# Attention stage of an attention, mixture-of-experts and MLP kernel: k laid out by depth, one product per pair of heads, and a new order of the stage

## The chip, the cores and the metric

The kernel runs on 1 core of one Trainium2 chip. The metric is the device time of one execution in microseconds (us). Engines have short names: PE is TensorE (PEld its weight loads), DVE is VectorE, ACT is ScalarE, POOL is GpSimd, SP is SyncE, which only issues transfers here.

## The reference, cut to what matters

```python
batch, n_heads, seq, head_dim = (8, 8, 576, 64)
...
def _attn_ref(q, k, v):
    q_s = np.exp(q - np.max(q, axis=-1, keepdims=True))
    q_s = q_s / (np.sum(q_s, axis=-1, keepdims=True) + 1e-09)
    k_s = np.exp(k - np.max(k, axis=2, keepdims=True))
    k_s = k_s / (np.sum(k_s, axis=2, keepdims=True) + 1e-09)
    kv = np.einsum('bhsd,bhse->bhde', k_s, v)
    return np.einsum('bhsd,bhde->bhse', q_s, kv)
...
x = attention output as 4608 tokens x 512
x = moe(x)        # 8 experts, each token goes to the one with the largest gate
out = moe2(x)     # 512 -> 2048 -> 512 with a leaky activation
```

q is normalised over the depth of a head (64), k over the sequence (576). The two large products after it (the experts, then the last MLP) take most of the time; the change touches the attention stage alone.

## The kernel before, in words

The attention stage is the function `attention`. Two batches make a pair, so there are 4 pairs of 1152 tokens, and a pair is 9 chunks of 128 tokens (4 of the first batch, 4 of the second, and one with the last 64 tokens of each). 8 heads of 64 are 4 pairs of heads (`hp`) of 128 columns. `j` is the batch inside the pair.

Per pair of batches the steps are these (lines of the kernel before). Loads: `load_k`, `load_v`, `load_q` (L125 to L138), on SP's queue, with tokens on the partitions. Maximum of k over the sequence: `kmax` (L149 to L151) takes elementwise maxima of the token chunks on DVE, `kmax_t` (L156) transposes the result on PE, `kmax_m` reduces it (L160) and makes diagonal matrices on ACT (L164), `kmax_b` multiplies by ones on PE (L170) so that every partition holds the maximum, copies it out on ACT (L172), and subtracts it from k in place, on POOL (L175, L176) but for one half of pair 0 on DVE. `kexp` (L180, L183) is exp on ACT in place. `kv` (L192) multiplies the five token chunks of a batch and a pair of heads with v; two columns of ones behind v give the sums. `kvn` (L198 to L207) divides by them and writes two diagonal blocks of 64x64 into a persistent tile `kvx`. `kvT` and `kg` (L214 to L224) multiply these blocks by the gate's weights, so that the gate's logits come out of the same product as the attention. For q: `qmax` (L245) and `qsub` (L249) by thirds of a pair, on DVE, the third `qsub` of pairs 1 to 3 on POOL. Per chunk: `trans` (four transposes L260, exp on ACT L262), `xmm` (product with `kvx`, L273 or L278, sums and logits taken out on ACT L280, L281, reciprocal on DVE L282), `evac` (division on DVE L287, store to `xd`). After a pair, `phase_r` finds each token's expert in 17 small steps r0 to r16 on DVE, and `scat` (L384) scatters a row per token into `region` with 36 indirect DMAs of POOL in all, 9 per pair (the last pair in 6 and 3).

The order of the stage is written out: every step has a due time in the table `TIMES`, a pair has a period of 12.5, the steps of all pairs are sorted by due time and issued in that order, and each engine works its own instructions in that order. The work on k's maximum, difference and exp for a pair lies two periods ahead of its x products, the products with v one period ahead.

After the stage `slot_tables` counts tokens per expert on DVE, `idload` (L552) reads the first 512 rows of `region`, which needs all scatters, and the experts begin.

```python
a1 += [at(i, f"kmax{j}", kmax, j), at(i, f"kmax_t{j}", kmax_t, j), at(i, f"kmax_m{j}", kmax_m, j),
       at(i, f"kmax_b{j}", kmax_b, j, eng)]
...
add(i - 2, a1)
add(i - 1, a2)
add(i - 1, phase_q(i))
add(i, phase_b(i))
...
for x in sorted(steps, key=lambda x: x[:2]):
    x[2](*x[3:])
```

Of the kernel before, what the change touches and what calls it, by code (L numbers as in the profile page):

```python
# [9 lines left out]
F32 = mybir.dt.float32  # L10
# [3 lines left out]
AF = mybir.ActivationFunctionType  # L14
# [8 lines left out]
NPAIR = B // 2  # L23
# [38 lines left out]
def lay_qk(a):  # L62
    r = np.ascontiguousarray(a.transpose(0, 2, 1, 3)).reshape(NT, DM)
    return np.ascontiguousarray(r[token_order()].transpose(0, 2, 1, 3))


def lay_v(a):
    r = a.transpose(0, 2, 1, 3).reshape(NPAIR, 2, S, 4, 128)
    o = np.zeros((NPAIR, 128, 2, 5, 4, 130), np.float32)
    for j in range(2):  # L70
        m = r[:, j, :512].reshape(NPAIR, 4, 128, 4, 128)
        o[:, :, j, :4, :, :128] = m.transpose(0, 2, 1, 3, 4)
        o[:, :, j, :4, :, 128:] = 1.0
        o[:, 64 * j:64 * j + 64, j, 4, :, :128] = r[:, j, 512:]
        o[:, 64 * j:64 * j + 64, j, 4, :, 128:] = 1.0
    return o
# [17 lines left out]
def attention(ctx, tc, cst, a, region, xd):  # L94
# [21 lines left out]
    T = cst["times"]  # L116

    def on(p, key, default):
        return {"p": nc.gpsimd, "v": nc.vector, "a": nc.scalar}[T.get((p, "E" + key), default)]

    def at(p, key, fn, *args):
        return (T.get((p, key), T[key]), fn) + args


    def load_k(i):  # L125
        t = kt[i] = kp.tile([128, NC, DM], F32, tag="k", name=f"k{i}")
        nc.sync.dma_start(out=t[:, 0:4], in_=a["k"][i, :, 0:4])
        nc.sync.dma_start(out=t[:, 4:9], in_=a["k"][i, :, 4:9])

    def load_v(i):  # L130
        t = vt[i] = kp.tile([128, 2, 5, 4, 130], F32, tag="v", name=f"v{i}")
        for j in range(2):
            nc.sync.dma_start(out=t[:, j], in_=a["v"][i, :, j])

    def load_q(i):
        t = qt[i] = kp.tile([128, NC, DM], F32, tag="q", name=f"q{i}")
        for c in range(0, 9, 3):
            nc.sync.dma_start(out=t[:, c:c + 3], in_=a["q"][i, :, c:c + 3])  # L138

    def phase_a(i):  # L140
# [3 lines left out]
        def kmax(j):  # L144
            pm2 = sp.tile([128, 2, DM], F32, tag="pm2", name="pm2", bufs=1)
            pm = s["pm", j] = sp.tile([128, DM], F32, tag="pm", name="pm")
            kj = kt[i][:, 4 * j:4 * j + 4]
            r = slice(64 * j, 64 * j + 64)
# [4 lines left out]
        def kmax_t(j):  # L153
            tp = s["tp", j] = ps_k.tile([128, 4, 128], F32, tag="kv", name="tp")
            for hp in range(4):
                nc.tensor.transpose(out=tp[:, hp], in_=s["pm", j][:, 128 * hp:128 * hp + 128], identity=ident)  # L156

        def kmax_m(j):
            m = sp.tile([128, 4], F32, tag="m", name="m")
            nc.vector.tensor_reduce(out=m, in_=s["tp", j], axis=AX.X, op=ALU.max)  # L160
            dg = s["dg", j] = sp.tile([128, 4, 128], F32, tag="dg", name="dg")
            if on(i, f"kmax_m{j}", "a") is nc.scalar:
                for hp in range(4):
                    nc.scalar.activation(out=dg[:, hp], in_=ident, func=AF.Copy, scale=m[:, hp:hp + 1])  # L164
            else:
                nc.vector.tensor_tensor(out=dg, in0=bc(ident, 1, 4), in1=bc(m[:, :], 2, 128), op=ALU.mult)

        def kmax_b(j, eng):
            mp = ps_k.tile([128, DM], F32, tag="kv", name="mp")
            nc.tensor.matmul(mp, lhsT=onesf, rhs=s["dg", j].rearrange("p a b -> p (a b)"), start=True, stop=True)  # L170
            mb = sp.tile([128, DM], F32, tag="mb", name="mb")
            nc.scalar.copy(out=mb, in_=mp)  # L172
            kj = kt[i][:, 4 * j:4 * j + 4]
            r = slice(64 * j, 64 * j + 64)
            eng.tensor_tensor(out=kj, in0=kj, in1=bc(mb[:, :], 1, 4), op=ALU.subtract)  # L175
            eng.tensor_tensor(out=kt[i][r, 8], in0=kt[i][r, 8], in1=mb[r], op=ALU.subtract)  # L176

        def kexp(j, half):
            kj = kt[i][:, 4 * j + 2 * half:4 * j + 2 * half + 2]
            nc.scalar.activation(out=kj, in_=kj, func=AF.Exp)  # L180
            if half == 1:
                r = slice(64 * j, 64 * j + 64)
                nc.scalar.activation(out=kt[i][r, 8], in_=kt[i][r, 8], func=AF.Exp)  # L183

        def kv(j, hp):
            half, g = hp // 2, hp % 2
            if g == 0:
                s["kvp", j, half] = ps_k.tile([128, 2, 130], F32, tag="kv", name="kvp")
            kvp = s["kvp", j, half]
            for c in range(5):  # L190
                kc = 8 if c == 4 else 4 * j + c
                nc.tensor.matmul(kvp[:, g], lhsT=kt[i][:, kc, 128 * hp:128 * hp + 128], rhs=vt[i][:, j, c, hp],  # L192
                                 start=(c == 0), stop=(c == 4))

        def kvn(j, half):
            kx, kvp = kvx[(2 * i + j) % 4], s["kvp", j, half]
# [3 lines left out]
            for g in range(2):  # L200
                r = slice(64 * g, 64 * g + 64)
                if on(i, f"kvn{j}{half}", "a") is nc.vector:
                    nc.vector.tensor_tensor(out=kx[r, 2 * half:2 * half + 2, 64 * g:64 * g + 64],
                                            in0=kvp[r, :, 64 * g:64 * g + 64], in1=bc(rk[r], 2, 64), op=ALU.mult)
                    continue
                for h in range(2):
                    nc.scalar.activation(out=kx[r, 2 * half + h, 64 * g:64 * g + 64], in_=kvp[r, h, 64 * g:64 * g + 64],  # L207
                                         func=AF.Copy, scale=rk[r, h:h + 1])

        def kvT(j):  # L210
# [4 lines left out]
            t = s["kvT", j] = sp.tile([128, 4, 128], F32, tag="kvT", name="kvT", bufs=1)  # L215
# [904 lines left out]
```

## Time and profile before

| what | us |
|---|---|
| median of 3 runs | 1438.41 |
| lowest and highest of the runs | 1435.17, 1444.23 |
| the profiled execution's own time | 1432.66 |
| its span, first to last instruction | 1430.9 |
| first x product of pair 0 begins | 62.30 |
| first x product of pair 3 begins | 167.85 |
| first read of `region` for the experts | 207.63 |

The profiled execution is 5.75 us below the median of the runs and 2.51 us below the lowest. Times in the rows are counted from the span's start. A busy time is a sum over instructions; matmuls overlap, so that the start-to-start distance of two groups says more than their busy time.

### The profile page before, as it was taken

How to read it: one execution, taken by the hardware profiler on the slowest of the kernel's cores; microseconds unless marked ns; L12 is line 12 of the kernel's file. 1: busy time of each engine (PE TensorE's matmuls, PEld its weight loads, DVE VectorE, ACT ScalarE, POOL GpSimd, SP SyncE). 2: the span in 40 equal slices, each digit the busy share in tenths (PEclk: the TensorE clock that was granted, in tenths of full speed). 3: DMA queues.
4: the chain of work that ended last, by engine and by line, in shares of the span. 5: the costliest groups of instructions: out<-in, count | busy, mean ns of one | idle time of the engine just before them, and what ended most of it. 6: DMA issues, size and time to landing. Idle time of an engine off the chain costs nothing.

```text
span 1430.9 us, 23212 instructions
## 1 busy us (share of the span) xinstructions
PE 1310.8 (92%) x9083; PEld 1215.1 (85%) x9083; DVE 1036.2 (72%) x1371; ACT 601.7 (42%) x946; POOL 342.7 (24%) x257
## 2 busy tenths in 40 slices
PE   4787817999999999998999999999989999999998
PEld 2677816787778777878899999999989999999998
DVE  5677755777777777755677777877768877777775
ACT  3566504555455545556233233323324333434332
POOL 2447451001110111011233333343421111110111
PEclk9899967999999999999999999999999999999999
DMA  9545227688878877696953323333496434434330
GB/s 372 218 193 199 104 79 258 222 277 256 264 235 272 268 254 248 216 315 205 352 204 139 122 101 136 148 118 148 187 421 217 132 122 145 139 124 135 120 118 31
DMA packets 144664, 279.54 MB, mean 195 GB/s; under 512 B 17952, under 2 KB 70176, under 8 KB 141600
## 3 DMA queue, kind: packets, MB, share of 16 engines
q1 hardware_dynamic: 119760, 208.45, 42.9%
q10 hardware_dynamic: 17232, 48.48, 8.6%
q0 software_dynamic: 7552, 21.02, 4.1%
q8 instruction: 74, 1.21, 0.4%
q14 instruction: 46, 0.38, 0.1%
HBM read 181.59 MB, written 96.32 MB: 194 GB/s over the span
## 4 chain that ended last, share of the span: by engine, by line
issue 26%; DVE 9%; PE 8%; POOL 6%; DMA 2%; ACT 1%; POOLq 0%; SPq 0%; DVEq 0%; ACTq 0%
PE hp L807 8%; POOL out L988 3%; POOL s L847 2%; DMA wi<-wid 2%; DVE ht L820 1%; DVE ht L856 1%; DVE ht L853 1%; DVE s L844 1%; DVE ht L840 1%; DVE x L488 1%; DVE s L842 1%; POOL s L848 1%; DMA hd<-ht 1%; DVE xl L488 0%; DVE xt L795 0%
## 5 line engine op out<-in xcount | busy, mean ns | idle before, releaser
L807 PE MATMUL hp<-xh,wi 128*128 128x256 f32 x1152 | 213.1, 281 | 4.9 <-DVE ht L856 2.3
L966 PE MATMUL yp<-wi,x 128*128 128x256 f32 x1152 | 191.2, 283 | 0.8 <-DVE x L488 0.8
L807 PEld LDWEIGHTS hp<-xh,wi 128*128 128x128 f32 x1152 | 179.5, 188 | 7.7 <-DVE ht L856 3.5
L966 PE MATMUL yp<-wi,wi 128*128 128x256 f32 x1200 | 178.3, 283 | 0.5 <-DVE wi L488 0.3
L807 PE MATMUL hp<-x,wi 128*128 128x256 f32 x1296 | 163.9, 285 | 7.7 <-DVEq L714 6.2
L807 PEld LDWEIGHTS hp<-x,wi 128*128 128x128 f32 x1296 | 160.2, 194 | 8.2 <-ACTq L714 6.4
L966 PEld LDWEIGHTS yp<-wi,wi 128*128 128x128 f32 x1200 | 163.5, 192 | 0.9 <-DVE wi L488 0.5
L966 PEld LDWEIGHTS yp<-wi,x 128*128 128x128 f32 x1152 | 161.5, 192 | 1.0 <-DVE x L488 1.0
L807 PE MATMUL hp<-xl,wi 128*128 128x256 f32 x576 | 160.7, 279 | 0.0
L559 POOL DMA_INDIRECT xg<-xd,idi x44 | 55.7, 1265 | 398.4 <-DVE hl L581 349.1
L578 PE MATMUL hp<-xh,w1h 128*128 128x512 f32 (+1 forms) x320 | 123.4, 386 | 11.2 <-DVE hl L581 10.3
L589 PE MATMUL yp<-hh,w2h 128*128 128x512 f32 (+1 forms) x320 | 122.9, 384 | 0.0
L988 POOL DMA_INDIRECT out<-yo,idx x36 | 47.4, 1316 | 315.1 <-DVE idx L982 294.4
L578 PE MATMUL hp<-xh,w1l 128*128 128x512 f32 (+1 forms) x320 | 121.9, 381 | 0.0
L578 PE MATMUL hp<-xl,w1h 128*128 128x512 f32 (+1 forms) x320 | 121.9, 381 | 0.0
L589 PE MATMUL yp<-hl,w2h 128*128 128x512 f32 (+1 forms) x320 | 121.5, 380 | 0.0
L589 PE MATMUL yp<-hh,w2l 128*128 128x512 f32 (+1 forms) x320 | 121.4, 379 | 0.0
L488 DVE TENSOR_TENSOR w1l<-st,w1h 128x1024 fp32r<-128x1024 f32 x44 | 53.7, 1226 | 76.7 <-ACT w1h L487 74.4
L807 PEld LDWEIGHTS hp<-xl,wi 128*128 128x128 f32 x576 | 108.0, 187 | 0.0
L820 DVE SCALAR_TENSOR_TENSOR ht<-ht 128x1024 f32<-128x1024 f32 x72 | 104.8, 1456 | 2.5
L847 POOL TENSOR_TENSOR s<-s,s 128x512 f32<-128x512 f32 x36 | 48.3, 1341 | 208.7 <-DVE s L844 160.8
L849 ACT ACTIVATE ht<-s 128x512 f32<-128x512 f32 x36 | 22.8, 633 | 149.7 <-POOL s L848 145.1
(210 smaller groups left out, 2615.1 us busy)
## 6 DMA issues: line engine op xcount, KB each, us to landing
st<-in_w SPq DMA_DIRECT2D x89, 512.0 KB
hd<-ht ACTq DMA_DIRECT2D x72, 512.0 KB
xt<-hd SPq DMA_DIRECT2D x18, 1024.0 KB
hr<-hd SPq DMA_DIRECT2D x18, 1024.0 KB
wi<-wid SPq DMA_DIRECT2D x28, 512.0 KB
wi<-wod SPq DMA_DIRECT2D x6, 2048.0 KB
v<-in_v SPq DMA_DIRECT2D x8, 1300.0 KB
q<-in_q SPq DMA_DIRECT2D x12, 768.0 KB
```

The source lines that it names most:

```text
L488: nc.vector.tensor_tensor(out=lo, in0=src, in1=hi.bitcast(F32), op=ALU.subtract)
L559: nc.gpsimd.indirect_dma_start(out=xg[:, t], out_offset=None, in_=xd, in_offset=bass.IndirectOffsetOnAxis(ap=idi[:, t:t + 1], axis=0), bou ...
L578: nc.tensor.matmul(hp[:, rows], lhsT=w[:, k, 128 * f:128 * f + 128], rhs=x[:, k, rows], start=(n == 0), stop=(n == 11))
L589: nc.tensor.matmul(yp[:, rows], lhsT=w[:, f, 128 * d:128 * d + 128], rhs=h[:, f, rows], start=(n == 0), stop=(n == 23))
L807: self.nc.tensor.matmul(bank[:, g], lhsT=w[:, h, k, 128 * g:128 * g + 128], rhs=x[:, k], start=(n == 0), stop=(n == 5))
L820: V.scalar_tensor_tensor(out=c, in0=c, scalar=0.01, in1=c, op0=ALU.mult, op1=ALU.max)
L840: V.tensor_tensor(out=h[:, 0, 0], in0=bank, in1=s[1], op=ALU.add)
L842: V.tensor_tensor(out=s[6], in0=bank, in1=s[1], op=ALU.add)
L847: G.tensor_tensor(out=s[6], in0=s[6], in1=s[5], op=ALU.add)
L849: nc.scalar.activation(out=h[:, 1, 1], in_=s[5], func=AF.Relu)
L966: nc.tensor.matmul(bank, lhsT=x[:, k], rhs=w[i][:, h, k], start=(c == 0), stop=(c == 23))
L988: ins = nc.gpsimd.indirect_dma_start(out=out, out_offset=bass.IndirectOffsetOnAxis(ap=idi[s % 2][:, t:t + 1], axis=0), in_=y[:, t], in_off ...
```

## The change

k comes laid out with depth on the partitions and the sequence along the free axis: for a pair of batches and a pair of heads, 128 partitions (two heads of 64) by 1152 tokens of both batches. The maximum is one `tensor_reduce` per pair of heads, the difference two `tensor_scalar` with the maximum as a number per partition. PE then transposes the difference in nine pieces of 128x128 into PSUM, in three tiles (4, 4 and 1 pieces) of the pool `ps_t` that the transposes of q use as well, and ACT applies exp on the way out. v is laid out by pairs of heads; k and v are loaded in four pieces of one pair of heads each. A product tile `kvp` holds both batches of one pair of heads, so `kvn` runs per pair of heads and its addition of 1e-9 moves from ACT to DVE. The reciprocal of the x sums moves from `xmm` to `evac`. All of `qsub` is on DVE. The table goes; the due times are written in the code, a period is 9 (one unit per chunk), and all work on a pair's k and q lies one period ahead of its x products. The routing steps and the scatters have new places too: those of a pair come behind r16, at 6.7 of the next period.

```diff
-        def kmax(j):
...
-            nc.vector.tensor_tensor(out=pm2, in0=kj[:, 0:2], in1=kj[:, 2:4], op=ALU.max)
-            nc.vector.tensor_tensor(out=pm, in0=pm2[:, 0], in1=pm2[:, 1], op=ALU.max)
-            nc.vector.tensor_tensor(out=pm[r], in0=pm[r], in1=kt[i][r, 8], op=ALU.max)
...
-            eng.tensor_tensor(out=kj, in0=kj, in1=bc(mb[:, :], 1, 4), op=ALU.subtract)
...
+        def kmax(hp):
+            m = sp.tile([128, 2], F32, tag="m", name="m", bufs=3)
+            nc.vector.tensor_reduce(out=m, in_=kt[i][:, hp].rearrange("p (j t) -> p j t", j=2), axis=AX.X, op=ALU.max)
+            for j in range(2):
+                k = kt[i][:, hp, S * j:S * j + S]
+                nc.vector.tensor_scalar(out=k, in0=k, scalar1=m[:, j:j + 1], scalar2=None, op0=ALU.subtract)
+
+        def kexp(hp, n):
...
+            n = (0, 2, 1)[n]
+            w = 1 if n == 1 else 4
+            tp = ps_t.tile([128, 4, 128], F32, tag="t", name="tk")
+            for c in range(w):
+                k0 = (0, 512, 640)[n] + 128 * c
+                nc.tensor.transpose(out=tp[:, c], in_=kt[i][:, hp, k0:k0 + 128], identity=ident)
+            nc.scalar.activation(out=ek[:, (0, 8, 4)[n]:(0, 8, 4)[n] + w], in_=tp[:, 0:w], func=AF.Exp)
...
-            nc.scalar.activation(out=rk, in_=kvp[:, :, 128], func=AF.Identity, bias=eps[:, 0:1])
+            nc.vector.tensor_scalar(out=rk, in0=kvp[:, :, 128], scalar1=1e-9, scalar2=None, op0=ALU.add)
...
+        l = []
+        for hp in range(4):
+            l += [(2 * hp - 1.95, kmax, hp)] + [(2 * hp - 0.8 + 0.02 * n, kexp, hp, n) for n in range(3)]
+            l += [(2 * hp + 0.4 + 0.01 * j, kv, hp, j) for j in range(2)] + [(2 * hp + 1.02, kvn, hp)]
+        l += [(7.35 + 0.01 * j, kvT, j) for j in range(2)] + [(8.15 + 0.01 * j, kg, j) for j in range(2)]
...
-            nc.vector.reciprocal(out=ri[:, c], in_=ri[:, c])
 
         def evac(c):
             ri = st_b[i][1]
+            nc.vector.reciprocal(out=ri[:, c], in_=ri[:, c])
...
+            l += [(c - 0.9, trans, c), (c + 0.3, xmm, c), (c + 1.0, evac, c)]
...
     for i in range(NPAIR):
...
+        add(NC * (i - 1), phase_k(i) + phase_q(i))
+        add(NC * i, phase_x(i))
+        if i < 2:
+            t0 = -100 + 10 * i
+            add(t0, [(t, load_kv, i, hp) for hp, t in enumerate((0, 1, 3, 4))] + [(t, load_q, i, n) for n, t in enumerate((2, 5, 6))])
+        else:
+            t0 = NC * (i - 2)
+            add(t0, [(0.5 * hp, load_kv, i, hp) for hp in range(4)] + [(7.9, load_q, i, n) for n in range(3)])
...
+    for i in range(NPAIR - 1):
+        route(NC * (i + 1), i, 0, NC, spread, 6.7)
...
-TIMES = {'kmax0': 0.52, 'kmax_t0': 2.07, 'kmax_m0': 2.08, 'kmax_b0': 2.81, 'kexp00': 5.69, 'kexp01': 5.14, 'kmax1': 2.61, ...
```

In the order of instructions the change shows first on DVE at the start of the program. `k_133` and `q_139` are k and q of pair 0, `m` the maximum, `rk` the reciprocal sums of k, `qm` the maximum of q. Before:

```order
L106 MEMSET eps 128x1
L149 TENSOR_TENSOR pm_153<-k_133 128x1024
L150 TENSOR_TENSOR pm<-pm_153 128x512
L151 TENSOR_TENSOR pm<-pm,k_133 64x512
L160 TENSOR_REDUCE m<-tp 128x4
```

Now, the same place:

```order
L111 MEMSET eps 128x1
L140 TENSOR_REDUCE m<-k_133 128x2
L143 TENSOR_SCALAR k_133<-k_133,m 128x576 x2
L140 TENSOR_REDUCE m<-k_133 128x2
L143 TENSOR_SCALAR k_133<-k_133,m 128x576 x2
L167 TENSOR_SCALAR rk<-kvp 128x2
L168 RECIPROCAL rk<-rk 128x2
L206 TENSOR_REDUCE qm<-q_139 128x24
L140 TENSOR_REDUCE m<-k_133 128x2
L143 TENSOR_SCALAR k_133<-k_133,m 128x576 x2
L210 TENSOR_TENSOR q_139<-q_139,qm 128x1536
```

DVE's maximum of two whole loads of k, with a return to it after PE, has become a maximum and a difference per pair of heads; the first `rk`, which waits for the product of the first pair of heads, stands ahead of the third pair's maximum.

The second place is PE between x products of pair 0, where `xp` is the x product (a row of 4 is a chunk), `kvp` the product with v for pair 1, `tq` a transposed chunk of q, `tp<-cf,pm` and `mp` the transposes and the product for the maximum of pair 2's k. Before:

```order
L273 MATMUL xp<-kvx_117,eq 128x146 x4
L156 MATMUL tp<-cf,pm 128x128 x4
L192 MATMUL kvp<-v_146,k_143 128x130 x5
L260 MATMUL tq<-cf,q_139 128x128 x8
L170 MATMUL mp<-dg,cf 128x512
L273 MATMUL xp<-kvx_117,eq 128x146 x4
L192 MATMUL kvp<-v_146,k_143 128x130 x5
```

Now, with `tk` the transposed difference of pair 1's k:

```order
L220 MATMUL tq<-cf,q_139 128x128 x4
L154 MATMUL tk<-cf,k_147 128x128 x9
L233 MATMUL xp<-kvx_117,eq 128x146 x4
L220 MATMUL tq<-cf,q_139 128x128 x4
L233 MATMUL xp<-kvx_117,eq 128x146 x4
L161 MATMUL kvp<-v_148,ek 128x130 x10
L220 MATMUL tq<-cf,q_139 128x128 x4
L154 MATMUL tk<-cf,k_147 128x128 x9
```

Between two products with v PE now has nine transposes of k, each group of which waits for DVE's difference and leaves through ACT; the work for the pair after next is gone from here.

## Rows read from the trace of the kernel before

**Rows 1.** Busy time per engine by stretch: core us, busy us (x), clock, DMA.
```profile
0.00:62.30 62.30, 33.49 (x150) 26.46 (x151) 36.48 (x39) 27.41 (x61) 23.45 (x22) 0.87 0.82 327
62.30:99.45 37.15, 31.41 (x234) 28.61 (x234) 29.12 (x37) 23.93 (x70) 17.18 (x5) 0.95 0.31 118
99.45:139.11 39.66, 30.19 (x236) 27.30 (x235) 30.06 (x56) 24.10 (x72) 22.89 (x11) 0.99 0.64 244
139.11:167.85 28.74, 26.43 (x214) 25.09 (x214) 20.26 (x47) 15.52 (x55) 16.87 (x14) 0.96 0.27 100
167.85:207.63 39.78, 15.44 (x113) 13.90 (x111) 25.02 (x106) 8.21 (x31) 17.75 (x18) 0.77 0.21 66
```

**Rows 2.** Instructions in order of time: first x product of pairs 0 and 3, read of `region`.
```profile
62.30 2.43 PE L273 MATMUL xp<-kvx,eq 128*128 128x146 f32 x16
...
167.85 2.16 PE L273 MATMUL xp<-kvx,eq 128*128 128x146 f32 x16
...
207.63 0.00 SPq L552 DMA_DIRECT2D idt<-region  x1
```

**Rows 3.** Busy time by stretch as in rows 1, for the start.
```profile
0.00:10.00 10.00, 0.00 (x0) 0.00 (x0) 2.55 (x7) 1.18 (x1) 3.35 (x16) 1.00 0.83 311
10.00:20.00 10.00, 4.70 (x11) 2.56 (x12) 4.79 (x7) 3.24 (x10) 2.84 (x1) 1.00 0.96 362
20.00:30.00 10.00, 6.00 (x22) 4.12 (x20) 7.30 (x10) 6.03 (x8) 2.87 (x2) 1.00 1.00 410
```

**Rows 4.** Instructions in order of time at the start: DVE's first, and PE's first product with v.
```profile
8.26 1.22 DVE L149 TENSOR_TENSOR pm<-k 128x1024 f32<-128x1024 f32 x1
...
24.58 2.07 PE L192 MATMUL kvp<-v,k 128*128 128x130 f32 x8 [3.16 <-issue]
```

**Rows 5.** Instructions in order of time: PE in the period of pair 2.
```profile
145.87 1.04 PE L260 MATMUL tq<-cf,q 128*128 128x128 f32 x8
...
147.27 1.24 PE L273 MATMUL xp<-kvx,eq 128*128 128x146 f32 x8
...
148.35 1.28 PE L192 MATMUL kvp<-v,k 128*128 128x130 f32 x10
...
163.36 1.77 PE L278 MATMUL xp<-kvx,eq 128*64 128x146 f32 x16
...
165.06 1.06 PE L222 MATMUL kg<-wg,kvT 128*128 128x8 f32 x8
```

**Rows 6.** Groups by line, 62.30 to 99.45: count | busy us, mean ns | idle before.
```profile
L249 DVE TENSOR_TENSOR q<-q,qm 128x1536 f32<-128x1536 f32 x2 | 8.7, 4340 | 0.0
L287 DVE TENSOR_TENSOR xr<-xp,ri 128x512 f32<-128x512 f32 x9 | 6.1, 682 | 0.7 <-DVE ri L282 0.6
L245 DVE TENSOR_REDUCE qm<-q 128x24 f32<-128x1536 f32 x3 | 5.2, 1742 | 0.0
L262 ACT ACTIVATE eq<-tq 128x512 f32<-128x512 f32 x9 | 5.2, 598 | 0.4 <-PE tq L260 0.3
...
L207 ACT ACTIVATE kvx<-kvp,rk 64x64 f32<-64x64 f32 x16 | 4.1, 303 | 1.8 <-DVE rk L199 1.7
...
L149 DVE TENSOR_TENSOR pm<-k 128x1024 f32<-128x1024 f32 x2 | 2.4, 1195 | 0.0
...
L282 DVE RECIPROCAL ri<-ri 128x8 f32<-128x8 f32 x9 | 1.8, 196 | 12.6 <-ACT ri L280 12.5
...
L150 DVE TENSOR_TENSOR pm<-pm 128x512 f32<-128x512 f32 x2 | 1.4, 692 | 0.1
```

**Rows 7.** Groups by line, whole span: a tensor_scalar in fp32.
```profile
L625 DVE TENSOR_SCALAR r<-r 128x1024 f32<-128x1024 f32 x16 | 11.1, 695 | 0.6
```

**Rows 8.** Instructions in order of time: a difference of q without POOL beside it.
```profile
154.33 1.75 DVE L249 TENSOR_TENSOR q<-q,qm 128x1536 f32<-128x1536 f32 x1
```

**Rows 9.** Instructions in order of time: POOL's scatters at the end, first and last of 14.
```profile
187.92 0.97 POOL L384 DMA_INDIRECT region<-tg,ix  x1 [6.94 <-issue]
...
204.76 0.97 POOL L384 DMA_INDIRECT region<-tg,ix  x1 [0.30 <-issue]
```

More of the change, by code (lines that the diff above doesn't have):

```diff
@@ L115, in attention @@
     kt, vt, qt, st_b = {}, {}, {}, {}
[L116 to L133, printed above, removed]
@@ L197, in kvn @@
             rk = sp.tile([128, 2], F32, tag="rk", name="rk")
-            nc.scalar.activation(out=rk, in_=kvp[:, :, 128], func=AF.Identity, bias=eps[:, 0:1])
+            nc.vector.tensor_scalar(out=rk, in0=kvp[:, :, 128], scalar1=1e-9, scalar2=None, op0=ALU.add)
             nc.vector.reciprocal(out=rk, in_=rk)
[L200 to L208, printed above, removed]
+            for j in range(2):
+                for g in range(2):
+                    r = slice(64 * g, 64 * g + 64)
+                    nc.scalar.activation(out=kvx[(2 * i + j) % 4][r, hp, 64 * g:64 * g + 64], in_=kvp[r, j, 64 * g:64 * g + 64],
+                                         func=AF.Copy, scale=rk[r, j:j + 1])
@@ L245, in qmax, with qsub, phase_x @@
             nc.vector.tensor_reduce(out=qm, in_=heads(n), axis=AX.X, op=ALU.max)
-        def qsub(n, eng):
+        def qsub(n):
             v = heads(n)
-            eng.tensor_tensor(out=v, in0=v, in1=bc(s[n][:, :], 2, D), op=ALU.subtract)
-        eng = [on(i, f"qsub{n}", "p" if i and n == 2 else "v") for n in range(3)]
-        return [at(i, f"qmax{n}", qmax, n) for n in range(3)] + [at(i, f"qsub{n}", qsub, n, eng[n]) for n in range(3)]
-    def phase_b(i):
+            nc.vector.tensor_tensor(out=v, in0=v, in1=bc(s[n][:, :], 2, D), op=ALU.subtract)
+        return [(t, qmax, n) for n, t in enumerate((1.5, 3.5, 6.5))] + [(t, qsub, n) for n, t in enumerate((2.5, 5.5, 8.5))]
+    def phase_x(i):
         s = {}
@@ L390, in phase_r, with add @@
         fs = [r0, r1, r2, r3, r4, r5, r6, r7, r8, r9, r10, r11, r12, r13, r14, r15, r16]
-        return [(f"r{m}", f) for m, f in enumerate(fs)] + [(f"scat{c}", scat, c) for c in range(n)]
-    for i in range(2):
-        load_k(i)
-        load_v(i)
-        load_q(i)
-    last = NPAIR - 1
+        return fs, [(scat, c) for c in range(n)]
     steps = []
-    def add(period, l):
+    def add(t0, l):
         for x in l:
-            steps.append((PERIOD * period + x[0], len(steps)) + tuple(x[1:]))
+            steps.append((t0 + x[0], len(steps)) + tuple(x[1:]))
@@ new lines, in route @@
+    def route(t0, i, c0, c1, times, ts):
+        fs, scats = phase_r(i, c0, c1)
+        add(t0, [(t, f) for t, f in zip(times, fs)] + [(ts + 0.001 * n,) + x for n, x in enumerate(scats)])
+    spread = [1.6, 2.6, 3.6, 3.61, 3.62, 3.63, 3.64, 4.6, 4.61, 4.62, 4.63, 4.64, 5.05, 5.06, 5.07, 6.6, 6.61]
+    for i in range(NPAIR - 1):
+        route(NC * (i + 1), i, 0, NC, spread, 6.7)
+    t0 = NC * NPAIR
+    route(t0, NPAIR - 1, 0, LASTC, [-2.9, -2.8] + [-1.9 + 0.01 * n for n in range(7)] + [-1.8, -1.79, -1.78] + [-0.95 + 0.01 * n for n in range(5)], -0.5)
```

119 lines of the change are left out of this document (37 added, 82 removed).

## The prediction, made before the changed kernel ran

> **What bounds the kernel now.** I read the busy time by stretch first, cut where the first x product of a pair begins, and looked for the first read of `region`, because the experts wait for it. The reader is to see that the stage is a chain of five stretches [rows 1]: 62.30 us until the first x product, three periods of 37.15, 39.66 and 28.74, and 39.78 from pair 3's first x product to the read at 207.63 [rows 2]. What comes behind is unchanged work, so I count only when that read moves.
>
> In the first stretch PE is busy for 33.49 of 62.30. In the three periods it is busy for 31.41, 30.19 and 26.43, so it stands idle for 5.74, 9.47 and 2.31, on average 5.84; DVE is busy for 29.12, 30.06 and 20.26 [rows 1]. Both are near a bound there and wait for one another: of DVE's idle time in the first period 12.5 us stand ahead of the reciprocal of the x sums, which DVE reaches before PE and ACT have the sums [rows 6]. In the last stretch all engines are half idle; its end belongs to POOL, whose last 14 scatters follow each other from 187.92 to 204.76, one each (204.76 - 187.92) / 13 = 1.295 us, and the read comes 2.87 behind the last one's start [rows 2, 9].
>
> **The change part by part: the start.** Before, DVE begins at 8.26, works on whole loads, and PE begins its first product with v at 24.58, each matmul taking 2.07 / 8 = 0.26 us; later ten take 1.28, so 0.13 each [rows 4, 5]. That is the lower of PE's two levels (1.2 and 2.4 GHz), although the row of that stretch gives a clock of 1.00 [rows 3]. Now k comes in pieces. A quarter of k is 128 x 1152 x 4 bytes = 0.59 MB, of v 0.67 MB, a third of q 0.79 MB. By the rates of rows 3 (311, 362, 410 GB/s) 3.1 MB are there at 10 us, 6.7 at 20 and 10.8 at 30; the order of loads is k and v of two pairs of heads, q, two pairs, q, q. So k of the second pair is there at about 9, of the fourth at about 18, the second third of q at about 21. DVE's queue rules, not the loads:
> - A maximum is 1742 x 1152 / 1536 = 1.31 us by qmax, which is the same instruction [rows 6]. A difference is 0.39, from the `tensor_scalar` of 1024 numbers at 0.695 [rows 7]; at most 0.67, by the two-source form at 1195 ns for 1024 [rows 6]. Together 2.1 per pair of heads (bound 2.65).
> - The first is done at 10.5. Three groups of transposes at the lower level (9 x 0.26) overlap exp at 0.60 [rows 6]; the first twenty matmuls with v run from about 12.6 to 17. DVE has done the second maximum at 12.6 and now waits for them, because the first `rk` stands ahead of the rest of its queue.
> - From 17.0 DVE has two more maxima (4.2), two differences of q (3.5 by rows 8), three maxima of q (5.2, rows 6), four `rk` pairs (1.2) and six small instructions for the bias (1.9, an estimate of 0.3 each, somewhat over the reciprocal's 196 ns [rows 6]): 16.0, so 33. PE follows inside that time.
> - Then in turn: scaling on ACT (1.1), transposes and copy of `kvx` (1.3, the copy taken like an exp of 512), the gate product (2.1 by rows 5, copies 0.5), nine transposes with exp (2.1), and the next four of q: 8. The first x product begins at **41**, 21.3 earlier than 62.30. If DVE did not have to wait for `rk`, 37; with PE at the lower level throughout (6.8 per pair of heads instead of DVE's pace), 46.
>
> **The periods.** PE's list for one pair: 8 chunks at 1.08 (148.35 - 147.27), the ninth 1.77, eight products with v at 1.12 (1.28 less what overlaps, as 1.24 stands to 1.08), 72 + 8 transposes at 0.13, gate products 2 x 1.06 [rows 5]: 8.6 + 1.8 + 9.0 + 10.4 + 2.1 = 31.9 us. 36 of these transposes are new, 4.7 us; the 8 transposes and two products of the old maximum go. So PE has more to do than in any period of before. I add the average idle time of before, 5.84: a period of **37.7**, three make 113.1, against 105.55 before (37.15 + 39.66 + 28.74). That is a loss of 7.6; most of it is that the period of pair 2 did not have the early part of a later pair's k, which now every period has.
>
> DVE for one pair, from its 29.12 [rows 1]: less the old maxima (2.4 and three groups of 1.4, L150 and two alike, 6.6), less what the differences of q cost beside POOL (8.7 for two, now three at 1.75: 3.4 [rows 6, 8]), plus four maxima 5.2, eight differences 3.1 and four additions 0.8: 28.2; with some fifteen small routing steps of 0.2 in the periods of pairs 1 and 2 about 31. It stays a little under PE. The reciprocal now comes 0.7 of a unit after its product in the order, so the 12.5 us wait should mostly go.
>
> The Trainium skill, VectorE: DVE Perf Modes, section on mode 2x_2P, says that a `tensor_scalar` with one fp32 source in SBUF works two elements at a time, and a two-source instruction cannot. The trace agrees in that 1024 numbers take 0.695 against 1.195. Were the form with one maximum per partition denied it, DVE would have 2.2 us more per period, 33 in all, still under 37.7, and the sum would stay.
>
> ACT: 23.93 of 37.15 is busy [rows 1]. Even if all twelve new exps (at most 0.60 each, 7.2) were added and nothing taken, 31.1 fit. They hide behind PE unless they come late at a group of transposes; that price is a rival below. The loads of k and v for pairs 2 and 3 stand on SP's queue around the first stores of x, 5 MB, some 13 us at 400 GB/s; four buffers of x rows (four units, 16 us) cover that. Without the cover the fifth division would wait, some 3 us a period. POOL loses its differences of k and q and keeps the scatters; those of pairs 0 and 1 are hidden.
>
> **The end.** Pair 2's routing is ready behind the sixth division of pair 3 and two routing steps (1.4). By about 2 us a unit that is 14 after the first x product. From there POOL has 18 scatters: the last begins 17 x 1.295 = 22.0 later, and the read 2.87 after that: 14 + 22.0 + 2.9 = **38.9** against 39.78. Bounds: 37 if a unit takes 1.6, 42 if it takes 2.5.
>
> **Sum.** 41 + 113.1 + 38.9 = 193.0 against 207.63: 14.6 earlier. On the profiled execution's own 1432.66 that gives 1418.0. The median of the runs is 5.75 above this execution and its lowest run 2.5; I go half the way to the median and forecast **1421**, which on 1438.41 is 1.2% and on equal footing (14.6 of 1432.66) 1.0%.
>
> **Rivals.**
> - A, lockstep: PE and DVE now have 32 and 28 to 31 us of work in one order, each behind the other's results. If every period has the idle time of pair 1's, 9.47, it is 41.4, three are 124.1, and the read comes at 204.0: 3.6 earlier, 1429. For it: that period had the routing and a full k, as all but the first now have. Against: its differences of k and q collided with POOL (4340 ns instead of 1750 [rows 6, 8]), and DVE stood at the reciprocal.
> - B, the slower side: the transposes of k, of q and the routing's small product share two PSUM buffers, and each group frees its buffer only when ACT has done its exp. Twelve groups of k a period are new, 36 in the three periods. If ACT, in order behind `kvx` scalings (16 in 4.1 us) and exps, is late by 0.9 us more per group than the idle time I added contains, that is 32 us: 1450. It eats the gain from 14.6 / 36 = 0.41 us per group and makes the kernel slower by 1% from 0.8. For it: PE's queue is in order, and nine transposes stand right ahead of an x product. Against: the transposes of q went the same way with only 0.4 us of idle time before nine exps, most of it ACT waiting for PE [rows 6].
> - C, better: PE's idle time falls to that of pair 2's period, 2.31, since POOL is out of the way: 34.2 a period, 102.6, the read at 182.5, 25 earlier: 1407.5. Against: DVE was at 20 of 29 us there and is now at 31.
>
> The Trainium skill, TensorE: Matmul & The Clock Gate, Part 1, says that PE's clock follows how busy it has been of late. In this trace PE is at 0.95 to 0.99 in the periods with 76 to 92% busy, and at 0.77 in the last [rows 1]. By the rule a PE that is busy from 10 us on would leave the lower level earlier than before, and one that waits for DVE at each pair of heads would stay there; these are the 41 and the 46 above.
>
> **How the numbers follow.** Forecast (gain of 7 to 22) 0.58, A 0.18, B 0.12, C 0.12. A measurement of this kernel tells about 1% from no change. Faster by over 1% are C and the upper part of the forecast (0.36): 0.48. Within 1%: the rest of the forecast (0.22), A, and the mild end of B (0.03): 0.43. Slower: 0.09. The range runs from C's 1407, reached with a start of 41 and periods of 34.2, to 1439, where the bad bounds meet: a start at 46, three periods of 41.4 and an end of 42 put the read at 212.1, 4.5 later than before, so 1437 on this execution and 1440 with the same half shift; B's full price lies outside. The forecast's own range is 1411 to 1428.
>
> **What would show it.** Right: the first x product at 38 to 46; the three periods 35 to 40 each with DVE over 75% busy; hardly any wait of DVE at the reciprocal; differences of q at 1.75 throughout; POOL's last 18 scatters without a gap; the rest of the span unchanged. Wrong: a first x product later than 50, or waits of PE for `ek` or `tk` of over 10 us per period (B), or a time behind the read that differs by more than 3 us, since then the change acts where I did not look.

## The result, and the profile after

The changed kernel is 1.2% slower: 1456.38 us, median of 4 runs, against 1438.77 for the kernel before, median of 4 as well; ratio 1.0121, 95% interval 1.0083 to 1.0158. Its profiled execution took 1454.22, with a span of 1452.5. The forecast was 1421, with a range that ended at 1439.

The busy time of the changed kernel by stretch, cut where the first x product of a pair begins and at the read of `region`, as in [rows 1] (columns: stretch and its length; busy us and instructions of PE, PEld, DVE, ACT, POOL; PE's granted clock; DMA share; GB/s):

```profile
0.00:41.72 41.72, 23.49 (x158) 21.72 (x159) 27.30 (x43) 15.24 (x39) 3.36 (x16) 0.92 0.97 378
41.72:85.45 43.73, 35.22 (x259) 32.97 (x257) 24.64 (x40) 20.40 (x61) 0.00 (x0) 0.88 0.54 212
85.45:131.10 45.65, 35.19 (x261) 33.06 (x260) 32.33 (x65) 20.59 (x63) 7.37 (x6) 0.89 0.58 214
131.10:177.11 46.01, 36.14 (x252) 33.86 (x251) 30.08 (x61) 18.93 (x58) 10.12 (x10) 0.85 0.15 53
177.11:227.87 50.76, 18.33 (x117) 16.57 (x115) 27.44 (x109) 9.15 (x34) 19.47 (x20) 0.70 0.17 53
```

The start went as forecast (41.72 for 41). The three periods are 43.7, 45.7 and 46.0 where 37.7 was forecast, and the end is 50.8 instead of 38.9. The read comes at 227.87, after 207.63 in [rows 2]; what lies behind it is 1224.6 against 1223.3, so the change acts in the stage alone.

What the engines waited for, between the first x products of pairs 0 and 3 (engine and line, releaser: us in sum, times, longest), first in the changed kernel:

```profile
DVE ri L245 <- ACT ri L240: 32.8, 12, 4.9
ACT kvx L172 <- DVE rk L168: 27.8, 7, 6.0
...
PE tk L154 <- ACT eq L222: 24.8, 9, 5.2
...
ACT kvx L172 <- PE tq L220: 7.0, 3, 2.4
ACT kvx L172 <- DVE oh L328: 6.2, 2, 3.3
```

and in the kernel before, over the same three periods:

```profile
DVE ri L282 <- ACT ri L280: 20.7, 11, 8.9
...
ACT kvx L207 <- DVE rk L199: 7.4, 12, 2.9
...
PE tq L260 <- ACT eq L262: 3.1, 2, 2.7
```

One wait is new: PE stands at the second group of k transposes (`tk`) for 24.8 us in 9 waits. Another has grown: ACT stands at the scaling of `kvx`, for 27.8 us in 7 waits by the row for `rk` where the kernel before has 7.4 in 12. The view puts the other five scalings under other releasers (7.0 and 6.2 us), but in the trace each of the 12 begins 0.09 to 0.11 us after the end of its `rk`, so that ACT's wait for `rk` is 41.0 us in 12. The changed kernel's instructions in order of time, at one of the 9 places, show that they are one chain (start, duration, engine, line, operation; in brackets the idle time before it and its releaser):

```profile
50.67 2.40 PE L161 MATMUL kvp<-v,ek 128*128 128x130 f32 x20
50.68 1.34 DVE L140 TENSOR_REDUCE m<-k 128x2 f32<-128x1152 f32 x1
...
52.05 0.95 DVE L143 TENSOR_SCALAR k<-k,m 128x576 f32<-128x576 f32 x2
...
52.92 1.75 DVE L210 TENSOR_TENSOR q<-q,qm 128x1536 f32<-128x1536 f32 x1
...
53.34 0.60 PE L154 MATMUL tk<-cf,k 128*128 128x128 f32 x4
...
55.34 0.69 DVE L247 TENSOR_TENSOR xr<-xp,ri 128x512 f32<-128x512 f32 x1 [0.56 <-DVE ri L245]
55.95 0.15 DVE L167 TENSOR_SCALAR rk<-kvp 128x2 f32<-128x2 f32 x1
...
56.39 1.28 ACT L172 ACTIVATE kvx<-kvp,rk 64x64 f32<-64x64 f32 x4 [5.16 <-DVE rk L168]
57.70 0.60 ACT L222 ACTIVATE eq<-tq 128x512 f32<-128x512 f32 x1
...
58.35 1.33 PE L154 MATMUL tk<-cf,k 128*128 128x128 f32 x5 [4.41 <-ACT eq L222]
...
59.47 2.15 PE L233 MATMUL xp<-kvx,eq 128*128 128x146 f32 x8
```

PE is through with the products with v at 53.07. The two tiny instructions of `rk` that read them stand in DVE's order behind a maximum of k, two differences of k, a difference of q, a reciprocal and a division, and begin at 55.95. ACT's next instruction is the scaling that needs `rk`; the exps of `tq` and `tk`, whose inputs have been ready since 53.5 and 53.9, stand behind it. They hold both shared PSUM buffers, so PE has nowhere to put the next group of k and waits 4.41 us. Then it runs at the lower of its two levels: the five transposes take 1.33, the eight x products 2.15, where eight take 1.24 in [rows 5].

Against the rows of before: a maximum takes 1.34 (forecast 1.31 from [rows 6]); a difference of k 520 ns (the trace's median) where 0.39 was worked out from [rows 7]; a difference of q 1.75 throughout, as in [rows 8] and not the 4.3 of [rows 6].

### The profile page after: what moved, and what is told of

The parts are those of the page before. It is cut to its first block, busy times and chain, and to the rows that moved or that the text cites. A ratio compares the mean times of both kernels' runs of the same rounds, so it can differ in the third digit from the quotient of the medians.

```text
span 1452.5 us, 23422 instructions
## 1 busy us (share of the span) xinstructions
PE 1321.0 (91%) x9179; PEld 1231.9 (85%) x9179; DVE 1036.8 (71%) x1404; ACT 586.7 (40%) x914; POOL 285.1 (20%) x240
## 4 chain that ended last, share of the span: by engine, by line
issue 25%; PE 8%; DVE 8%; POOL 6%; DMA 3%; ACT 1%; POOLq 0%; SPq 0%; DVEq 0%
PE hp L765 8%; POOL out L946 3%; DMA wi<-wid 2%; POOL s L805 2%; DVE ht L778 1%; DMA hd<-ht 1%; DVE ht L814 1%; DVE ht L811 1%; DVE x L446 1%; DVE s L802 1%; DVE ht L798 1%; POOL s L806 1%; DVE s L800 1%; DVE xl L446 0%; ACT ht L807 0%
## 5 line engine op out<-in xcount | busy, mean ns | idle before, releaser
L536 PE MATMUL hp<-xh,w1h 128*128 128x512 f32 (+1 forms) x320 | 122.9, 384 | 12.0 <-DVE hl L539 11.5
```

The lines of the kernel that those rows point to most:

```text
L536: nc.tensor.matmul(hp[:, rows], lhsT=w[:, k, 128 * f:128 * f + 128], rhs=x[:, k, rows], start=(n == 0), stop=(n == 11))
```

## The experiments

**Theory T1**: the chain above, an in-order queue on ACT whose head waits for a small instruction that stands late in DVE's order. Rivals: two buffers are too few in any case (R2), the clock or the amount of work alone (R3, R4), POOL and DVE hindering one another (R5). The experiments ran on two chips. The second profile of the kernel before, `rk` earlier, the late maximum and the early routing on top of it ran on one of them, all others on the other one. The kernel before takes 1428 to 1430 us on both, so totals are told as ratios to it; figures expected in us are for the first result, where it takes 1438.8. Ratios times 1428.6 give the differences below.

**Both kernels again.** No edit.

> The changed kernel itself, once more, as the yardstick of this group of runs and for a second profile. Expected: 1.2% over the kernel before, three periods of 130 to 140 us in sum and PE's waits for tk behind eq of 20 to 30 us. If the stalls of ACT with no releaser in the trace (5.4 and 4.8 us in the last stretch) and the slow slot tables belong to the kernel, they come again; if they are accidents of one execution, the last stretch is 3 to 8 us shorter here.

> The kernel before, once more, for a second profile on the chip of this group. Expected: the read of the region at 200 to 208 us, so that the three periods and the end of before can be set beside those of the changed kernel's second profile (read at 218.35); if before's stage is as in its first profile (105.55 in the periods, 39.78 in the end), the changed kernel's loss lies in the periods alone.

Measured: the changed kernel 1.0118 (1.0098 to 1.0137); the kernel before 1428.76. The changed kernel's second profile, the three periods and the end:

```profile
40.98:84.35 43.37, 34.86 (x258) 32.74 (x257) 24.64 (x40) 20.40 (x61) 0.00 (x0) 0.88 0.56 218
84.35:131.58 47.23, 36.71 (x260) 34.29 (x259) 32.44 (x65) 20.60 (x63) 8.33 (x8) 0.86 0.56 207
131.58:179.05 47.47, 36.63 (x251) 34.33 (x250) 30.16 (x62) 19.30 (x60) 9.11 (x9) 0.82 0.15 51
179.05:218.35 39.30, 15.93 (x116) 14.28 (x115) 26.99 (x108) 9.07 (x32) 19.69 (x21) 0.76 0.21 68
```

The same of the kernel before:

```profile
61.19:98.49 37.30, 31.56 (x233) 28.76 (x233) 29.13 (x37) 23.96 (x70) 17.19 (x5) 0.94 0.30 114
98.49:135.12 36.63, 29.79 (x236) 26.88 (x235) 29.88 (x56) 24.10 (x72) 19.91 (x10) 1.00 0.58 222
135.12:162.22 27.10, 25.34 (x215) 23.97 (x213) 20.79 (x48) 15.54 (x56) 19.59 (x15) 1.00 0.45 163
162.22:200.57 38.35, 16.71 (x113) 14.75 (x111) 25.00 (x106) 8.19 (x31) 18.01 (x19) 0.75 0.22 69
```

The two profiles come from two chips, on which the kernel before takes the same time (medians 1428.41 and 1428.65). By them the changed kernel gains 20.2 at the start (40.98 against 61.19), loses 37.0 in the periods (138.1 against 101.0) and 1.0 in the end: the read comes 17.8 later. The loss is in the periods. The long end of the first profile (50.8) did not come again; here it is 39.3. The 37.0 lost have two halves by these rows: PE is busy for 21.5 us more (108.2 against 86.7) and idle for 15.5 more (29.9 against 14.3).

**The scaling later on ACT.**

```diff
-            ... + [(2 * hp + 1.02, kvn, hp)]
+            ... + [(2 * hp + (1.45 if hp < 3 else 1.15), kvn, hp)]
```

> Edit: only the due time of the scaling of the k-v sums (kvn) is moved from 1.02 to 1.45 units after the pair of heads (1.15 for the last pair of heads), so that on ACT the exps of the next q chunk and of the next pair's first k group stand ahead of it, and on DVE the next maximum of k. Theory T1 (ACT's queue head: the scaling waits for rk, which stands late on DVE, and the exps behind it hold the two shared PSUM buffers): PE's waits for tk behind eq in the three periods fall from 24.8 us to under 8, each period gets 4 to 7 us shorter (135.4 to about 115 to 122), the clock in them rises to 0.93 or more, total 1436 to 1444. Rival R2 (two PSUM buffers are too few whatever stands at ACT's head): the waits stay at over 18 us, total within 4 us of 1456. Rival R3 (the longer periods come from the lower clock alone, set by the amount of work): periods within 2 us of 135.4 in sum.

Measured: 1.0008 (0.9995 to 1.0021), 15.7 us under the changed kernel. PE's wait at the same line, over the three periods:

```profile
ACT kvx L172 <- DVE rk L168: 6.0, 4, 2.2
...
PE tk L154 <- ACT eq L222: 3.3, 8, 0.7
```

and at the place shown above, where the exps no longer stand behind the scaling:

```profile
54.45 0.60 ACT L222 ACTIVATE eq<-tq 128x512 f32<-128x512 f32 x1 [1.50 <-PE tq L220]
...
55.11 0.82 PE L154 MATMUL tk<-cf,k 128*128 128x128 f32 x5 [0.31 <-ACT eq L222]
...
55.76 1.16 PE L233 MATMUL xp<-kvx,eq 128*128 128x146 f32 x8
```

PE waits 0.31 instead of 4.41, and its five transposes take 0.82 instead of 1.33. The wait of 24.8 is down to 3.3 with the same two buffers, so R2 falls. The periods are 122.3 in sum instead of 138.1 with the same work, so R3 falls too; the sum is at the upper end of what T1 gave (122). Their clock did not rise to the 0.93 expected but in the third (0.85, 0.85, 0.95; 0.88, 0.86, 0.82 in the changed kernel): other waits remain.

**`rk` earlier on DVE, ACT's order as it was.**

```diff
-        def kvn(hp):
+        def kvr(hp):
...
+        def kvn(hp):
+            kvp, rk = s["kvp", hp], s["rk", hp]
...
-            ... + [(2 * hp + 1.02, kvn, hp)]
+            ... + [(2 * hp + 0.42, kvr, hp), (2 * hp + 1.02, kvn, hp)]
```

> Edit to the changed kernel: the two DVE instructions of rk are due right behind the products with v (0.42 instead of 1.02), so ahead of an evacuation and, for two of four pairs of heads, of a difference of q; the scaling on ACT stays at 1.02, at the same place in ACT's queue. T1 (ACT's scaling at the queue's head waits for an rk that stands late on DVE): ACT's wait for rk falls from 31 us to under 15 in the three periods, PE's wait for tk behind eq from 25 to under 15, total 6 to 15 us under the changed kernel, though PE's buffers and ACT's order are untouched. Rival R2' (the wait goes only if the scaling itself leaves the place ahead of the exps): within 4 us of the changed kernel. Rival (DVE then stands at rk for PE as it did at the reciprocal): 2 to 10 us slower.

Measured: 1.0009 (0.9999 to 1.0019), 15.6 us under the changed kernel, a little over what T1 gave. Waits over the three periods:

```profile
PE tk L154 <- ACT eq L225: 12.6, 9, 1.7
DVE rk L167 <- PE kvp L161: 12.1, 5, 3.8
...
ACT kvx L175 <- PE tq L223: 13.9, 6, 2.3
...
ACT kvx L175 <- DVE ri L248: 9.6, 4, 2.7
...
ACT kvx L175 <- DVE rk L168: 6.2, 2, 3.1
```

The fall of ACT's wait at `rk` from 31.2 to 6.2 is in part one of names: here too each of the 12 scalings begins about 0.1 us after its `rk`, and the wait in 12 is 29.7 us (the three rows of `kvx`), against 43.1 in the changed kernel's second profile. What went are the long waits: none is over 3.1, where the longest was 6.0.

Either end of the chain undone gives the same 16 us: the scaling moved away from ACT's head, or `rk` moved forward on DVE. That is T1, and R2' falls. The price of this second way also shows: DVE now waits 12.1 us at `rk` for PE.

**More work on DVE ahead of `rk`.**

```diff
+    junk = one.tile([128, 1024], F32, name="junk")
...
+            nc.vector.memset(junk, 0.0)
```

> Edit: a memset of 128 x 1024 numbers on DVE (0.6 to 1 us, into a tile that nobody reads) ahead of each of the 16 rk, so that each scaling on ACT finds its rk later by that much; the result stays the same. T1 (the path goes through rk at most of the 12 groups of the periods): each of the 12 costs most of its length, 6 to 12 us in the three periods, PE's waits for tk behind eq grow from 24.8 to over 30 us, total 1463 to 1470. Rival R2 (DVE has slack ahead of rk, the wait is due to the buffers): under 3 us, total 1455 to 1459.

Measured: 1.0206 (1.0182 to 1.0230), 12.6 us over the changed kernel. The memset takes 0.912 us; 12 stand in the three periods, 10.9 together, and the periods grew by 11.6 (149.7 against 138.1). PE's wait for `tk` went from 25.0 to 28.1, less than expected; 5.0 of the 11.6 are longer busy time of PE (113.2 against 108.2; its clock was 0.81 and 0.80 in the second and third period), the rest is other idle time. DVE has no slack ahead of `rk`.

**Less work on DVE, but not ahead of `rk`.**

```diff
-            nc.vector.tensor_tensor(out=v, ...
+            (nc.gpsimd if i and n == 2 else nc.vector).tensor_tensor(out=v, ...
```

> Edit: the third difference of q of pairs 1 to 3 goes back to POOL, where it takes 2.76 us beside 1.75 on DVE, nothing else. T1: DVE's list in a period gets 1.75 us shorter, but differences of q stand behind the maxima, not ahead of the rk that PE waits for, so little is gained: total within 4 us of the changed kernel. Rival R4 (DVE's amount of work, 28 to 32 us a period, sets the period): 4 to 6 us faster. Rival R5 (POOL and DVE slow each other as in the kernel before, where the same difference took up to 5.5 us on DVE): 3 to 8 us slower.

Measured: 1.0118 (1.0086 to 1.0150), no difference from the changed kernel. The differences of q, on DVE and on POOL (count, then ns min/median/max):

```profile
L210 DVE TENSOR_TENSOR q<-q,qm x9: 1737/1752/1755, 19.1 to 164.3; 128x1536 f32<-128x1536 f32 x9
...
L210 POOL TENSOR_TENSOR q<-q,qm x3: 2759/2783/2796, 75.5 to 184.5; 128x1536 f32<-128x1536 f32 x3
```

1.75 us less for DVE in each period bought nothing, 0.91 more ahead of each `rk` cost its whole length: the order counts, not the amount (R4 falls for the changed kernel's order). R5 falls by another row: POOL is busy for 0.00 us in the changed kernel's first period, and that period is 6.1 us longer than the kernel before's all the same (43.37 against 37.30). The rows here don't test it, for no difference on DVE ran beside one on POOL. What slowed some in the kernel before was not tried.

**The reciprocal back behind its product.**

```diff
         def xmm(c):
+            nc.vector.reciprocal(out=ri[:, c], in_=ri[:, c])
         def evac(c):
-            nc.vector.reciprocal(out=ri[:, c], in_=ri[:, c])
```

> Edit: the reciprocal of the x sums stands again right behind its product in the written order (as before the change), not 0.7 of a unit later. T1 says that the periods are set by the scaling behind rk; an earlier reciprocal puts DVE at the head of its queue in front of PE and ACT, so rk comes later still: DVE's wait at the reciprocal grows from 40 to over 50 us, total 2 to 10 us over the changed kernel. Rival (the place of the reciprocal is free): within 2 us of it.

Measured: 1.0238 (1.0214 to 1.0263), 17 us over the changed kernel, more than expected. DVE's wait at the reciprocal and ACT's at the scaling (42.6 and 31.2 in the changed kernel's second profile):

```profile
DVE ri L242 <- ACT ri L240: 70.0, 14, 6.2
...
ACT kvx L172 <- DVE rk L168: 39.0, 8, 6.8
```

So the later reciprocal is a part of the change that pays, though DVE's wait there did not go.

**The end alone, and with the later scaling.**

```diff
-        route(NC * (i + 1), i, 0, NC, spread, 6.7)
+        route(NC * (i + 1), i, 0, NC, early if i == NPAIR - 2 else spread, 3.2 if i == NPAIR - 2 else 6.7)
```

> Edit: the due times of pair 2's routing steps in the last period are moved forward (its index at 3.1 units instead of 6.6, its scatters at 3.2 instead of 6.7), nothing else. Theory T2 (the end is 50.8 us and not 38.9 because the routing of pair 2 is queued behind the sixth division, and the 18 scatters begin 18.4 us after the first x product): the first of the last 18 scatters comes 5 to 9 us sooner, the stretch from pair 3's first x product to the read gets 4 to 8 us shorter, total 1448 to 1452. Rival T2b (the end is set by the slot tables on DVE behind the last index, not by the scatters): scatters come sooner, the read stays within 2 us of where it was, total 1454 to 1457.

> Edit: the two edits together, the late scaling of the k-v sums and the early routing of pair 2. T1 and T2 add up: read of the region 20 to 28 us sooner than in the changed kernel, total 1428 to 1438, so it beats the kernel before by 0 to 10 us. Rivals R2 and T2b: 1450 to 1456. If only one of the two holds, 1436 to 1450.

Measured: alone 1.0111 (1.0088 to 1.0134), within the interval of the changed kernel; together 1.0018 (0.9999 to 1.0037), no better than the later scaling by itself. T2 was built on the first profile's end, where the scatters begin 19.3 us after the x product (not 18.4); in the second it is 39.3, and the early routing made it 37.6: its scatters begin 2.6 us sooner and the read comes within 2 us of where it was, as T2b has it. T2 falls as the cause of any loss.

**The order spread over DVE.** From the later scaling on: the routing of pairs 0 and 1, and for pairs 1 to 3 two of the three maxima and two of the three differences of q, moved so that DVE's work does not bunch, and the routing's products on PE half a unit behind their casts.

```diff
-    spread = [1.6, 2.6, 3.6, ... 4.6, 4.61, 4.62, ... 5.05, 5.06, 5.07, 6.6, 6.61]
+    spread = [1.6, 3.6, 5.6, ... 6.6, 6.61, 6.62, 7.2, ... 7.9, 7.91, 7.92, 8.2, 8.21]
-        return [(t, qmax, n) for n, t in enumerate((1.5, 3.5, 6.5))] + [(t, qsub, n) for n, t in enumerate((2.5, 5.5, 8.5))]
+        return [(t, qmax, n) for n, t in enumerate((1.5, 5.5, 8.4) if i else (1.5, 3.5, 6.5))] + [(t, qsub, n) for n, t in enumerate((3.5, 6.5, 8.5) if i else (2.5, 5.5, 8.5))]
```

> Edit: the late scaling of the k-v sums as in the first experiment, and in the periods of pairs 1 and 2 the routing of the pair before, and the first two maxima and differences of q, moved so that no stretch between two evacuations has more than 4.4 us of DVE work; the routing's two small products on PE are due half a unit behind the casts that they read. In the first experiment PE still waited three times, 8.5 us in sum, for those casts. T1 in its general form (PE in order waits wherever DVE's written order bunches): these waits go, the second and third period fall from 44.5 and 37.8 to 38 to 41 and 35 to 38, total 3 to 8 us under the first experiment, so 0.2 to 0.5% under the kernel before. Rival R4 (DVE and PE are both full): periods as in the first experiment, within 2 us of it.

Measured: 0.9961 (0.9942 to 0.9979), 0.4% under the kernel before; the periods are 36.96, 40.66 and 33.24, 110.9 in sum instead of 122.3 with the same work, so R4 falls here as well. The parts of this edit were not tried apart. What still stood out was ACT waiting for `rk`, 8.0 us in 3 waits; in the first period it is the last `rk` of a pair, at 65.14, behind the next pair's first maximum and differences of k (62.90 to 65.23).

**That maximum behind the last `rk`**, and then the early routing too.

```diff
-            l += [(2 * hp - 1.95, kmax, hp)] + ...
+            l += [(2 * hp - (1.95 if i == 0 or hp else 1.8), kmax, hp)] + ...
```

> Edit to the version with the spread order: the first maximum and difference of k of a period is due at 7.20 units instead of 7.05, so behind the last rk of the pair before, which ACT waited for there (8.0 us in three waits). T1 in its general form: these waits and PE's wait for the transposes of kvx behind them (6.1 us) fall to under 4 each, the three periods get 2 to 6 us shorter in sum than 110.9, total 0.3 to 0.8% under the kernel before. Rival (the wait is moved to the first transposes of k): within 2 us of the spread order.

> Edit: that, and pair 2's routing early in the last period with its two products on PE half a unit behind their casts. POOL's last 18 scatters follow each other without a gap in the spread order (1.28 each), so the end of 39.3 should go to what pair 3's own routing allows: the first scatter 10 to 12 us after pair 3's first x product instead of 14, the read 2 to 4 us earlier, total 0.5 to 1.0% under the kernel before. Rival (the tail is bounded by pair 3's x products and its own routing): read within 1 us of the version without this edit.

Measured: 0.9841 (0.9820 to 0.9861), 1.6% under the kernel before and twice what was expected; ACT's wait for `rk` went from 8.0 to 3.8 us and PE's for the transposes of `kvx` from 6.1 to 1.9. With the early routing 0.9829 (0.9812 to 0.9845), no measurable difference: its read comes 0.6 us earlier, as the rival has it. The stretches of the version with the late maximum:

```profile
38.72:71.15 32.43, 30.94 (x257) 29.11 (x257) 24.54 (x40) 19.96 (x61) 0.00 (x0) 0.99 0.81 316
71.15:105.39 34.24, 31.14 (x260) 28.91 (x259) 31.86 (x65) 20.21 (x63) 2.21 (x2) 1.00 0.77 282
105.39:138.51 33.12, 30.11 (x252) 28.00 (x251) 29.52 (x62) 18.99 (x60) 10.87 (x10) 1.00 0.23 82
138.51:177.53 39.02, 16.84 (x117) 14.98 (x115) 28.00 (x110) 8.99 (x32) 25.88 (x26) 0.71 0.22 69
```

Where so much comes from is seen at the end of the first period: in the spread order the transposes of `kvx` waited, and PE fell to its lower level within the sixteen gate products behind them (granted clock 0.54 from 68 to 70 us, 0.50 from 70 to 74),

```profile
66.22 0.33 PE L179 MATMUL tp<-cf,kvx 128*128 128x128 f32 x1 [1.91 <-ACT kvx L172]
...
67.83 3.17 PE L187 MATMUL kg<-wg,kvT 128*128 128x8 f32 x16
...
73.04 2.68 PE L238 MATMUL xp<-kvx,eq 128*64 128x146 f32 x16
```

and with the late maximum they did not:

```profile
63.60 0.76 PE L179 MATMUL tp<-cf,kvx 128*128 128x128 f32 x4
...
65.64 1.88 PE L187 MATMUL kg<-wg,kvT 128*128 128x8 f32 x16
...
68.96 1.77 PE L238 MATMUL xp<-kvx,eq 128*64 128x146 f32 x16
```

Of the 11.1 us that the periods lost (110.9 to 99.8), 7.2 are PE's busy time (99.4 to 92.2) and 3.9 its idle time. From 138.1 to 99.8 the periods lost 38.3 us by due times alone, with the same instructions: 15.8 by the later scaling, 11.4 by the spread order, 11.1 by the late maximum. So the order made the loss, not the layout of k. PE's list with hardly a wait is 92.2 in the three periods; of the 21.5 us by which the changed kernel's busy time is over the kernel before's (108.2 against 86.7), 16.0 are therefore the lower level and 5.5 are left for the work that is new.

## Why the prediction was wrong, point by point

- **The start: right in sum, in part by luck.** 41.72 and 40.98 for 41, though a difference of k was sized at 0.39 and takes 0.52. In the second profile the first twenty products with v ended at 13.8 (forecast 17), and the way from the last `rk` took 6.4 (forecast 8). Against these stood two more waits of DVE at an `rk`, 2.8 and 1.4 us, which the forecast did not have. The chain of the periods shows here already: at 22.2 ACT had waited 5.31 us for an `rk` at its scaling, PE waited 4.46 for an exp behind that scaling, and PE's next twenty products with v took 4.54 instead of 2.40.
- **PE's list: right as a list.** 31.9 us was forecast; where PE hardly waits it is busy for 30.9, 31.1 and 30.1 a period (the late maximum). In the changed kernel's second profile the same list took 36.1 (108.2 / 3), because PE ran part of it at the lower level (its clock was 0.82 to 0.88, with the late maximum 0.99 to 1.00).
- **"I add the average idle time of before, 5.84": this step failed.** The idle time of one order was carried over to another. In the second profile it is 10.0 a period (29.9 / 3). In sum the periods are 138.1 instead of 113.1: 12.4 more idle time (29.9 against 17.5) and 12.5 more busy time (108.2 against 95.7). That is 25.0 of the 25.4 us by which the read came later than forecast (218.35 for 193.0). In the first profile, where it came at 227.87, 22.3 are the periods and 11.9 the end. Set beside the kernel before's own second profile the miss is 32.4 us (14.6 earlier was forecast, 17.8 later was measured), since the read of before comes there at 200.57 and not at 207.63.
- **The price of a wait was half left out.** The forecast counted a wait of PE at its length and put the lower level only into the bounds of the start. Behind the long waits the work that followed also ran at the lower level (granted clock 0.50 from 57 to 63 us in the second profile, behind a wait of 4.39), and in sum the longer busy time is as much again as the added idle time. The Trainium skill, TensorE: Matmul & The Clock Gate, section "HAM oscillation — how this bites in real kernels", describes PE waiting for transfers again and again and starting cold each time; the trace agrees for waits on an exp, with five transposes in 1.33 after a wait of 4.41 and in 0.82 after one of 0.31. Not every wait cost this. Of the nine in the second profile six were followed by work at the lower level and three (1.6, 1.6 and 2.3 us) were not; almost the same wait went either way:

```profile
90.92 0.82 PE L154 MATMUL tk<-cf,k 128*128 128x128 f32 x5 [2.30 <-ACT eq L222]
...
138.24 1.33 PE L154 MATMUL tk<-cf,k 128*128 128x128 f32 x5 [2.38 <-ACT eq L222]
```

  The product of the ninth chunk, too, ran at the lower level in each of the three periods (2.9 to 3.1 us for 1.77), with no wait of PE over 0.5 in the 10 us before it. What decides between the two levels there these runs don't show.
- **Rival B was right about the place and wrong about the reason.** The shared buffers and the exps behind the scalings are where PE waits. That its 1450 is near the 1456 measured is luck: it charged 0.9 us to each of 36 groups, and 9 of them waited, for 25.0 us in sum. ACT was not late by its own work, of which it has 19.3 to 20.6 us in 43 to 47; it stood at its head for an `rk` that DVE reached late. The prediction named DVE's wait for `rk` at the start and never asked, for the periods, what stands ahead of `rk` on DVE and behind the scaling on ACT. Its argument against B, the transposes of q in the kernel before, was drawn from an order in which ACT waits for its `rk` for 7.4 us in all, in 12 waits of at most 2.9. A chance of 0.12 was too low. The sign given for B, waits of over 10 us a period, was not reached either (8.3). None of the three signs of being wrong came; what showed it were signs of being right that stayed away: periods of 43.7 to 46.0 for 35 to 40, DVE busy for 56 to 71% of them for over 75%, and the wait at the reciprocal.
- **The exps on ACT, to "hide behind PE unless they come late"**: PE waited for one at 9 of the 36 groups, late by the order.
- **DVE: near in amount** (24.6 for 28.2 in the first period, 32.4 and 30.2 for about 31 in the others), and the amount did not matter. The wait at the reciprocal was to go; it is 42.6 where the kernel before has 22.1, yet the late reciprocal is worth 17 us. With the late maximum that wait is 7.4: it came from the order too.
- **The end: right in the second profile.** 39.3 for 38.9: the first of the 18 scatters 15.0 after the x product (forecast 14), then 22.0, then 2.3. The 50.8 of the first profile stays unexplained (below).
- **Its sums hold, but not on one footing.** The forecast of 1421 has half the way to the median (2.9) in it; the 1429 of A, the 1450 of B and the 1407.5 of C don't, and the range's end of 1439 lies between its 1437 and 1440. The 1456 measured is outside either way.
- **The gain was there.** With the order mended the read comes at 177.5, earlier than the 193.0 forecast, and the time is 1.6 to 1.7% under the kernel before: the layout of k is good, its table of due times was not.

## What to carry to other kernels

When a change gives a stage a new order, don't carry over the idle time of the old one: walk one repeat of it through each in-order queue, and for every short instruction ask what long ones stand ahead of it on its own engine, and what stands behind its reader on the next. Two tiny instructions at the wrong place cost 16 us here, and either end of the chain could be mended by due times alone. Count a wait of PE at more than its length wherever it brings the lower level, and mend the next wait too, since the last one mended here was worth about as much as the first (17.1 and 15.7 us by the ratios).

## What the runs showed of the hardware that was not expected

- Shifting one due time by 0.15 of a unit was worth 1.2% (0.9961 to 0.9841). Most of it is PE's level: its clock was 0.91, 0.87 and 1.00 in the three periods and then 0.99, 1.00 and 1.00, and 7.2 of the 11.1 us are busy time.
- In the first profile of the changed kernel ACT stood for 5.4 us with no releaser that the profile names on this core, just behind pair 2's last product, and again for 4.8 at 206.2:

```profile
181.02 0.27 ACT L240 ACTIVATE ri<-xp,eps 128x8 f32<-128x8 f32 x1 [5.38 <-remote]
```

  The second profile of the same kernel has no such stall there and an end shorter by 11.5 us: the first of the 18 scatters comes 15.0 after the x product instead of 19.3, and the read 2.3 behind the last one's start instead of 9.7. The cause stays open.
- A DVE memset of 128x1024 takes 0.912 us, longer than the `tensor_scalar` on as many numbers in [rows 7], and a `tensor_scalar` on 576 takes 0.52, not 576/1024 of 0.695.
